# Attention in written order: ScalarE evicts every transposed pair, one reciprocal and product per batch, bias tables on VectorE, more warming

## The chip, the cores and the metric

One core of one Trainium2 chip runs the whole program. The metric is the device time of one execution in microseconds (us); lower is better. Engines: PE is TensorE, PEld its weight loads, DVE VectorE, ACT ScalarE, POOL GpSimd, SP SyncE, which here only issues DMAs.

## The reference

Attention over q, k, v of shape (2, 8, 768, 64), then a soft mixture of experts on the 1536 x 512 tokens, then a top-2 mixture of 8 experts. The change touches attention alone:

```
scores = scale * q @ k^T - slope_h * dist
keep   = (key < 8) | (0 <= row - key < 96)
a      = exp(scores - max) where keep, else 0
a      = a / (sum(a) + 1e-9)
out    = a @ v
```

A query sees the 8 global keys and the 96 keys up to itself, so a tile of 128 queries needs its own 128 keys and the 95 before them.

## The kernel before

Work is cut into 12 tiles of 128 queries, T = 0 to 11 (six for each batch element; m = T % 6 counts within it). A tile has 4 pairs of heads, n = 4 T + p. A pair is worked in two halves t of 64 queries: 128 rows (two heads by 64 queries) by 167 keys (95 before, 8 global, 64 own). Two pairs are a batch i = 0 to 23; two batches are a tile. All in float32.

For a pair, `scores` (L194) multiplies on TensorE into a buffer of PSUM (two of them), and VectorE adds the bias table, scales and takes each row's minimum in one instruction per half (L205, the reduction). `exps` (L209): ScalarE's exponential with the row's sum, one per half. `norm` (L216): GpSimd adds 1e-9 to the sums of the pair (L219), VectorE takes the reciprocal (L220), GpSimd multiplies the 2 x 167 columns by it into the padded tile Pb (L223), and where m > 0 the 8 global columns once more (L225). `turn` (L227): TensorE transposes Pb in blocks of 128 x 128 into PSUM tile pt. `turned` (L236) evicts pt to PT: the first pair of a batch on ScalarE (L241), the second on VectorE (L243). `values` (L248): PT times v into px. `valued` (L262): ScalarE evicts px to xT (L266); GpSimd keeps the first 8 rows of v. `stX` (L272): TensorE transposes xT back (L276), VectorE evicts to xs (L282). Where m = 0 there is no earlier tile, and half the transposes and values fall away.

After tiles 3, 7, 10 and 11 a segment (`logits` L289, `seg` L297) adds the tiles to the first mixture's running sums: logits on TensorE (L293), their maximum on VectorE, Et = exp on ScalarE, transposes of Et and of the logits (L325, L326), and U's product (L349) and update (L353). `seg` is a generator: each `next` issues one more step.

Inside attention the order on TensorE, VectorE, ScalarE and GpSimd is written out by hand in `attention_near` (L384), and every engine follows its queue in order. Pass i of the loop (L394) issues in this order: loads; the VectorE eviction for batch i-2; scores and exponentials of batch i; stX of the tile before on even i; values of batch i-2; valued on odd i; logits; norm of batch i; transposes of batch i-1 and the ScalarE eviction. Steps of a running segment (s1, s2) stand between them.

SP issues the loads in the written order too: v for tile T+1, q for T+2, k for T+3 at each even pass, then pieces of the first mixture's weights (512 KB each, 32 in all) as `PACE` allows (L24: pieces issued by pass i). A load waits until the buffer that it fills is free: 3 for q, 4 for v. The next expert weights (L618) use the memory that attention gives back. The bias tables (slope times distance, for m = 0 and m > 0) are built before the loop: four pieces on ScalarE (L389), four on GpSimd (L391). `NWARM` matmuls on zeros run at the start (L132).

Of the kernel before, what the change touches and what calls it, by code (L numbers as in the profile page):

```python
# [57 lines left out]
def emit(tc, d, near=True, stop=None):  # L58
    nc = tc.nc
    es = ExitStack()  # L60
    with es:
# [52 lines left out]
        ps_l = pool("ps_l", 1, s_ps, space=PSUM)  # L114
        ps_o = pool("ps_o", 1, s_ps, space=PSUM)

        NQ, NP = 3 if near else 2, 4
        qd = [ac.tile([128, 4, 2, 128], F32, name=f"qd{i}") for i in range(NQ)]
        if near:
            kx = ac.tile([128, 4, KP + 6 * KS], F32, name="kx")  # L120
            bias = ac.tile([128, 2, 4, 2, 167], F32, name="bias")
            Pb = [ac.tile([128, 2, 264], F32, name=f"Pb{i}") for i in range(NP)]
            gvt = lo.tile([8, 512], F32, name="gv")
        phis = lo.tile([128, 4, 32], F32, name="phis")
        if near:
            for nm, shape in (("Tt", [128, 2, 167]), ("vt", [128, 512])):
                wk.tile(shape, F32, name=nm, bufs=4)
# [41 lines left out]
        if near:  # L169
            s_hand = ExitStack()  # L170
            s_hand.enter_context(tc.manual_schedule(engines=hands))
            zero32 = wz.bitcast(F32)

            def clear(i, eng):
                for h in range(2):
                    eng(qd[i][64 * h:64 * h + 64, :, 1 - h, :], zero32[64 * h:64 * h + 64, 0:128].unsqueeze(1).to_broadcast([64, 4, 128]))

            by_act = lambda o, z: nc.scalar.activation(o, z, AF.Copy)
# [12 lines left out]

        S = {}

        def scores(n, st, nm):  # L194
            T, p = divmod(n, 4)
            m = T % 6
            s = ps_s.tile([128, 2, 167], F32, name="s")
            qv = qd[T % NQ].rearrange("p a h (c t) -> p a t (h c)", t=2)
            for t in range(2):
                a = KS * m + 64 * t  # L200
                nc.tensor.matmul(s[:, t, :], qv[:, p, t, :], kx[:, p, a:a + 167], start=True, stop=True)  # L201
            Tt = wk.tile([128, 2, 167], F32, name="Tt", bufs=4)
            for t in range(2):
                k = 2 * (p % 2) + t
                nc.vector.tensor_tensor_reduce(Tt[:, t], s[:, t], bias[:, int(m == 0), p, t], -0.125, 1e30, ALU.add, ALU.min,  # L205
                                               nm[:, k:k + 1])
            S[n] = Tt

        def exps(n, st, nm):  # L209
            Tt = S[n]  # L210
            for t in range(2):
                k = 2 * (n % 2) + t
                nc.scalar.activation(Tt[:, t], Tt[:, t], AF.Exp, bias=nm[:, k:k + 1], scale=-1.0,  # L213
                                     accum_out=st[:, k:k + 1])

        def norm(n, st):  # L216
            Pu, k = S[n], 2 * (n % 2)
            r = sm.tile([128, 2], F32, name="r")
            nc.gpsimd.tensor_scalar(r, st[:, k:k + 2], 1e-9, None, ALU.add)  # L219
            nc.vector.reciprocal(r, r)  # L220
            Pn = Pb[n % NP]
            wide = lambda t, c, step, w: bass.AP(t[:, 0, c:c + 1].tensor, t[:, 0, c:c + 1].offset, [t.ap[0], [step, 2], [1, w]])
            nc.gpsimd.tensor_tensor(wide(Pn, 33, 264 + 64, 167), Pu, r.unsqueeze(2).to_broadcast([128, 2, 167]), ALU.mult)  # L223
            if n // 4 % 6:
                nc.gpsimd.tensor_tensor(Pn[:, :, 0:8], wide(Pu, 95, 167 - 64, 8), r.unsqueeze(2).to_broadcast([128, 2, 8]), ALU.mult)  # L225

        def turn(n):  # L227
            c0 = 0 if n // 4 % 6 else 1
            Pn = Pb[n % NP]
            pt = ps_t.tile([128, 2, 2, 128], F32, name="pt")  # L230
            for ch in range(c0, 2):
                for t in range(2):
                    nc.tensor.transpose(pt[:, ch, t], Pn[:, t, 136 * ch:136 * ch + 128], ident)  # L233
            S[n] = pt

        def turned(n, act):  # L236
            c0 = 0 if n // 4 % 6 else 1
            pt = S[n]
            PT = lo.tile([128, 2, 2, 128], F32, name="PT", bufs=2)
            if act:  # L240
                nc.scalar.activation(PT[:, c0:], pt[:, c0:], AF.Copy)  # L241
            else:
                nc.vector.tensor_copy(PT[:, c0:], pt[:, c0:])  # L243
            S[n] = PT

        X = {}

        def values(n):  # L248
            T, p = divmod(n, 4)
            m = T % 6  # L250
            PT = S.pop(n)
# [132 lines left out]
        def attention_near():  # L384

            NB = 24
            all_units()
            for p in range(4):
                nc.scalar.activation(bias[:, 1, p], dist[1], AF.Copy, scale=negs[:, p:p + 1])  # L389
            for p in range(4):  # L390
                nc.gpsimd.tensor_scalar(bias[:, 0, p], dist[0], negs[:, p:p + 1], None, ALU.mult)  # L391
            part = {}
            segs = {}
            for i in range(NB + 3):  # L394
                T, u = divmod(i, 2)
                old = segs.get(T - 3) if u else segs.get(T - 4 + 1)
                new = i < NB
                if new and u == 0 and T >= 2:
                    if T + 1 < NT:
# [15 lines left out]
                a, b = divmod(i - 5, 2)  # L415
                s1 = segs.get(a) if b == 0 else None
                a, b = divmod(i - 6, 2)
                s2 = segs.get(a) if b == 0 else None
                if s2:
                    list(s2)  # L420
                if s1:
                    next(s1)
                if new:
                    st, nm = [sm.tile([128, 4], F32, name=k, bufs=3) for k in ("st", "nm")]
                    for n in (2 * i, 2 * i + 1):
                        scores(n, st, nm)
                    exps(2 * i, st, nm)
                if s1:
                    next(s1)
                if new:  # L430
                    exps(2 * i + 1, st, nm)
# [9 lines left out]
                if s1:  # L441
                    next(s1)
                if new:
                    norm(2 * i, st)
                    norm(2 * i + 1, st)
                if 0 <= i - 1 < NB:
                    for n in (2 * (i - 1), 2 * (i - 1) + 1):
                        turn(n)
                    turned(2 * (i - 1), True)
# [4 lines left out]
                if s1:  # L454
                    next(s1)
                    next(s1)
            more_w(2 * (NWA + NW))
            psl = logits(*SEGS[NT - 1])
            stX(NT - 1)
# [1149 lines left out]
```

## Time and profile before

| what | value |
|---|---|
| median of 3 runs | 394.22 us (392.58 to 397.57) |
| profiled execution | 394.14 us, of which span 391.9 us |
| busy in the span | PE 325.3, DVE 207.5, ACT 203.5, POOL 154.1 us |
| mean granted clock of TensorE | 0.941 of full |

The span runs from the first to the last instruction; the execution's own time has 2.24 us around it. In an order of time, a row gives start, duration, engine, line, operation, what it writes and reads, a count where several rows were merged, and in brackets how long the engine stood idle before and who ended that. Durations of pipelined matmuls overlap, so the distance between two starts tells more than a duration. A row of windows gives each engine's busy time in the stretch and its instructions, the mean granted clock (1.00 is full speed), the busy share of the DMA engines and GB/s. A row of groups gives busy time, mean ns of one instruction, and idle time before them.

### The profile page before, as it was taken

The page shows a single profiled execution, that of the slowest core. Times are in us where ns is not written, and L with a number is a line of the kernel's source. Part 1 is how long each engine was busy: PE and PEld are TensorE (multiplying, and loading weights), DVE is VectorE, ACT ScalarE, POOL GpSimd, SP SyncE. Part 2 cuts the span into 40 slices and gives each one's busy share as a digit, 9 for nine tenths or more (in the row PEclk, how much of TensorE's full clock was granted, in tenths as well). Part 3 has the DMA queues.
Part 4 walks back from the last instruction along what each step waited for, and adds up shares of the span by engine and source line. Part 5 has one row for each costly group of instructions (what it writes and reads, how often), then busy time and mean ns, then how long its engine had stood idle before and what let it go on. Part 6 is the DMA issues. An engine that isn't in the chain of part 4 may idle for free.

```text
span 391.9 us, 7690 instructions
## 1 busy us (share of the span) xinstructions
PE 325.3 (83%) x2680; PEld 190.8 (49%) x2680; DVE 207.5 (53%) x770; ACT 203.5 (52%) x476; POOL 154.1 (39%) x254
## 2 busy tenths in 40 slices
PE   5598989897978999969779798999993499999920
PEld 3486767675854433436344344454541255544410
DVE  2355556655445200378959474947580475995100
ACT  4375665654642210456747757768462665775200
POOL 4866664563630000203821533543615332341231
PEclk8699999998999999989999899999998599999985
DMA  7999997998299999990767899889686983233442
GB/s 185 266 316 324 290 300 237 281 330 281 73 323 359 375 397 388 393 387 22 243 137 238 246 267 343 261 203 315 156 256 140 261 248 42 32 34 49 55 52 33
DMA packets 49515, 89.52 MB, mean 228 GB/s; under 512 B 3408, under 2 KB 18384, under 8 KB 49472
## 3 DMA queue, kind: packets, MB, share of 16 engines
q1 hardware_dynamic: 44992, 81.40, 62.9%
q0 software_dynamic: 4480, 7.57, 13.4%
q8 instruction: 23, 0.38, 0.4%
q14 instruction: 20, 0.16, 0.1%
HBM read 78.35 MB, written 10.62 MB: 227 GB/s over the span
## 4 chain that ended last, share of the span: by engine, by line
PE 47%; DVE 18%; DMA 12%; POOL 8%; issue 7%; ACT 5%; SPq 1%; POOLq 0%; DVEq 0%; ACTq 0%
PE y L1152 20%; PE y L699 4%; POOL Pb L223 3%; DMA out_y<-ys,sidx 3%; PE pg L653 3%; PE h L653 3%; DMA out_y<-w,sidx 2%; PE s L201 2%; DVE Tt L205 2%; PE h L1074 2%; DMA cT<-ctab,gidx 2%; PE px L259 2%; DVE hh L1083 2%; PE y L723 2%; ACT Tt L213 2%
## 5 line engine op out<-in xcount | busy, mean ns | idle before, releaser
L1152 PE MATMUL y<-w2hl,hh 128*128 128x512 f16 x552 | 128.4, 386 | 1.9 <-ACT hh L1075 1.9
L1152 PEld LDWEIGHTS <-hh 128*128 128x128 f16 x552 | 53.3, 99 | 65.2 <-issue 6.7
L213 ACT ACTIVATE Tt<-Tt,nm 128x167 f32<-128x167 f32 x96 | 40.5, 423 | 41.1 <-DVE nm L205 32.3
L1161 POOL DMA_INDIRECT out_y<-ys,sidx x16 | 27.2, 1698 | 64.0 <-ACT ys L1158 24.6
L1083 DVE SCALAR_TENSOR_TENSOR hh<-h,hh 128x512 f16<-128x512 f32 x46 | 29.6, 685 | 41.6 <-ACT hh L1075 41.6
L223 POOL TENSOR_TENSOR Pb<-Tt,r 128x334 f32<-128x334 f32 x48 | 35.7, 744 | 16.0 <-DVE r L220 15.0
L201 PE MATMUL s<-kx,qd 128*128 128x167 f32 x192 | 35.1, 331 | 2.9 <-DMA qd<-in_qt 2.9
L201 PEld LDWEIGHTS s<-kx,qd 128*128 128x128 f32 x192 | 31.3, 214 | 6.4 <-issue 6.2
L259 PE MATMUL px<-PT,vt 128*64 128x128 f32 x352 | 28.2, 287 | 5.2 <-DVE PT L243 4.1
L1161 POOL DMA_INDIRECT out_y<-c,sidx x8 | 15.7, 1960 | 42.9 <-ACT hh L1075 20.0
L220 DVE RECIPROCAL r<-r 128x2 f32<-128x2 f32 x48 | 7.9, 165 | 44.7 <-POOL r L219 44.6
L1075 ACT ACTIVATE hh<-h 128x512 f16<-128x512 f32 x46 | 24.9, 591 | 10.7 <-PE h L1074 10.7
L1171 POOL DMA_INDIRECT cT<-ctab,gidx x23 | 25.6, 1112 | 11.9 <-issue 5.5
L205 DVE CUSTOM_DVE_ANT_0 Tt<-s,bias 128x167 f32<-128x167 f32 x96 | 26.3, 327 | 7.2 <-ACT bias L389 5.9
L233 PE MATMUL pt<-c,Pb 128*128 128x128 f32 x176 | 25.4, 286 | 4.5 <-POOL Pb L223 4.5
L766 ACT ACTIVATE w2hl<-w 128x1024 f16<-128x1024 f32 x20 | 20.9, 1049 | 12.3 <-DMA w<-in_w2b 12.3
L259 PEld LDWEIGHTS px<-PT,vt 128*64 128x64 f32 x352 | 18.7, 138 | 13.2 <-DVE PT L243 8.2
L233 PEld LDWEIGHTS pt<-c,Pb 128*128 128x128 f32 x176 | 19.3, 144 | 8.9 <-POOL Pb L223 5.1
L780 ACT ACTIVATE w2hl<-w,pmw 128x1024 f16<-128x1024 f32 x19 | 20.9, 1142 | 3.2 <-DVE pmw L754 2.5
L786 DVE SCALAR_TENSOR_TENSOR w2hl<-w,pmw,w2hl 128x1024 f16<-128x1024 f32 x18 | 22.5, 1279 | 0.1
L219 POOL TENSOR_SCALAR r<-st 128x2 f32<-128x2 f32 x48 | 10.4, 218 | 20.0 <-ACT Tt L213 17.3
L1158 ACT ACTIVATE ys<-y,gsc 128x512 f32<-128x512 f32 x16 | 10.9, 683 | 14.0 <-PE y L1152 14.0
(280 smaller groups left out, 519.6 us busy)
## 6 DMA issues: line engine op xcount, KB each, us to landing
w<-in_w2b SPq DMA_DIRECT2D x10, 1024.0 KB, 6.3
w<-in_w1a SPq DMA_DIRECT2D x16, 512.0 KB, 7.3
w<-in_w2a SPq DMA_DIRECT2D x16, 512.0 KB, 6.6
w<-in_w1a SPq DMA_DIRECT2D x8, 1024.0 KB, 9.8
w<-in_w2a SPq DMA_DIRECT2D x8, 1024.0 KB, 13.1
w<-in_w1b SPq DMA_DIRECT2D x8, 1024.0 KB, 6.5
w2hl<-in_w1b SPq DMA_DIRECT2D x8, 1024.0 KB, 10.2
w2hl<-in_w2b SPq DMA_DIRECT2D x6, 1024.0 KB, 7.5
```

What stands on the lines that cost most here:

```text
L201: nc.tensor.matmul(s[:, t, :], qv[:, p, t, :], kx[:, p, a:a + 167], start=True, stop=True)
L205: nc.vector.tensor_tensor_reduce(Tt[:, t], s[:, t], bias[:, int(m == 0), p, t], -0.125, 1e30, ALU.add, ALU.min, nm[:, k:k + 1])
L213: nc.scalar.activation(Tt[:, t], Tt[:, t], AF.Exp, bias=nm[:, k:k + 1], scale=-1.0, accum_out=st[:, k:k + 1])
L223: nc.gpsimd.tensor_tensor(wide(Pn, 33, 264 + 64, 167), Pu, r.unsqueeze(2).to_broadcast([128, 2, 167]), ALU.mult)
L233: nc.tensor.transpose(pt[:, ch, t], Pn[:, t, 136 * ch:136 * ch + 128], ident)
L259: nc.tensor.matmul(px[64 * h:64 * h + 64, p, :], vv[:, c:c + 64], PT[:, ch, :, 64 * h:64 * h + 64], start=(ch == 0 or m == 0), stop=(ch == 1))
L653: nc.tensor.matmul(psum[32 * g:32 * g + 32, 0:n], lhs(k), rhs_of(k, g), start=(k == 0), stop=(k == nk - 1), tile_position=(0, 32 * g))
L1075: nc.scalar.activation(hh[:, 0, 4 * q:4 * q + 4], ph, AF.Relu)
L1083: nc.vector.scalar_tensor_tensor(hh[:, 1, 4 * q:4 * q + 4], phs[q], 0.0, hh[:, 0, 4 * q:4 * q + 4], ALU.max, ALU.subtract)
L1152: nc.tensor.matmul(py, hh[:, hx, f], w2hl[:, e, wx, f], start=(n == 0), stop=(n == 23))
L1161: nc.gpsimd.indirect_dma_start(out=out, out_offset=bass.IndirectOffsetOnAxis(ap=sidx[:, j:j + 1], axis=0), in_=ys, in_offset=None, compute ...
L1171: nc.gpsimd.indirect_dma_start(out=cg[n], out_offset=None, in_=ctab, in_offset=bass.IndirectOffsetOnAxis(ap=gidx[:, n:n + 1], axis=0))
```

## The change

All transposed pairs are evicted by ScalarE, right after their transposes in `turn`; xT is evicted by VectorE instead of ScalarE. A batch has one tile Tt of 4 x 167 columns (two buffers), one sum + 1e-9, one reciprocal of four columns and one product of 4 x 167 columns into one of two batch-wide Pb tiles. In a pass, the scores of both pairs come first, then four exponentials; the norm of batch i comes after the transposes of batch i-1. The steps of a segment are issued in the pass of its logits and the next one. The bias tables are built by VectorE, all but one piece, most of them after the first scores. 16 warming matmuls stand in place of 7, and 12 and 3 more in passes 1 and 2. An exponential on zeros is issued at the start. `PACE` gives 4 pieces in 3 passes in place of 3 in 2.

```
-NWARM = 7
+NWARM = 16
-PACE = lambda i: 1 + 3 * i // 2
+PACE = lambda i: 1 + 4 * i // 3
+FILL = {1: 12, 2: 3}
...
-        NQ, NP = 3 if near else 2, 4
+        NQ, NP = 3 if near else 2, 2
...
-            Pb = [ac.tile([128, 2, 264], F32, name=f"Pb{i}") for i in range(NP)]
+            Pb = [ac.tile([128, 4, 264], F32, name=f"Pb{i}") for i in range(NP)]
...
             nc.vector.memset(kx[:, :, 0:KP], 0.0)
+            nc.scalar.activation(sm.tile([128, 4], F32, name="st", bufs=3), zero32[:, 0:4], AF.Exp)
             clear(1, by_dve)
...
+        def scores(i, nm):
+            Tt = wk.tile([128, 4, 167], F32, name="Tt", bufs=2)
+            for n in (2 * i, 2 * i + 1):
...
+        def exps(i, st, nm):
+            Tt = S[i]
+            for k in range(4):
+                nc.scalar.activation(Tt[:, k], Tt[:, k], AF.Exp, bias=nm[:, k:k + 1], scale=-1.0,
                                      accum_out=st[:, k:k + 1])
...
+        def norm(i, st):
+            Pu = S[i]
+            r = sm.tile([128, 4], F32, name="r", bufs=3)
+            nc.gpsimd.tensor_scalar(r, st, 1e-9, None, ALU.add)
             nc.vector.reciprocal(r, r)
+            Pn = Pb[i % NP]
...
+            nc.gpsimd.tensor_tensor(wide(Pn, 33, 264 + 64, 528, 167), Pu.rearrange("p (a t) c -> p a t c", t=2), rb(167), ALU.mult)
+            if i // 2 % 6:
+                nc.gpsimd.tensor_tensor(Pn[:, :, 0:8].rearrange("p (a t) c -> p a t c", t=2), wide(Pu, 95, 167 - 64, 334, 8), rb(8), ALU.mult)
...
-        def turned(n, act):
...
+            PT = lo.tile([128, 2, 2, 128], F32, name="PT", bufs=2)
+            nc.scalar.activation(PT[:, c0:], pt[:, c0:], AF.Copy)
+            X["PT", n] = PT
...
-            nc.scalar.activation(X["xT", T], X["px"], AF.Copy)
+            nc.vector.tensor_copy(X["xT", T], X["px"])
...
-            for p in range(4):
-                nc.scalar.activation(bias[:, 1, p], dist[1], AF.Copy, scale=negs[:, p:p + 1])
-            for p in range(4):
-                nc.gpsimd.tensor_scalar(bias[:, 0, p], dist[0], negs[:, p:p + 1], None, ALU.mult)
+            def tables(m, a, b):
+                nc.vector.tensor_tensor(bias[:, m, a:b].rearrange("p a t c -> p a (t c)"),
+                                        dist[m].rearrange("p t c -> p (t c)").unsqueeze(1).to_broadcast([128, b - a, 334]),
+                                        negs[:, a:b].unsqueeze(2).to_broadcast([128, b - a, 334]), ALU.mult)
+            def fill(k):
+                for _ in range(k):
+                    nc.tensor.matmul(pw, wz[:, 0:128], wz, start=True, stop=True)
+            nc.scalar.activation(bias[:, 1, 0], dist[1], AF.Copy, scale=negs[:, 0:1])
+            tables(1, 1, 2)
...
-                if 0 <= i - 2 < NB:
-                    turned(2 * (i - 2) + 1, False)
...
+                s1 = segs.get(T - 2) if u else None
+                if new:
+                    st, nm = [sm.tile([128, 4], F32, name=k, bufs=3) for k in ("st", "nm")]
+                    scores(i, nm)
+                    exps(i, st, nm)
+                if i == 0:
+                    tables(1, 2, 4)
+                if i == 1:
+                    tables(0, 0, 2)
+                if i == 2:
+                    tables(0, 2, 4)
+                fill(FILL.get(i, 0))
                 if s1:
                     next(s1)
+                    next(s1)
                 if u == 0 and 0 <= T - 2 < NT - 1:
                     stX(T - 2)
                 if 0 <= i - 2 < NB:
...
                     if u:
                         valued(T - 1)
+                if s1:
+                    list(s1)
                 if u == 0 and T - 2 in SEGS and T - 2 < NT - 1:
                     segs[T - 2] = seg(*SEGS[T - 2], logits(*SEGS[T - 2]))
...
                 if 0 <= i - 1 < NB:
                     for n in (2 * (i - 1), 2 * (i - 1) + 1):
                         turn(n)
+                if new:
+                    norm(i, st)
+                if u == 0 and T - 2 in segs:
+                    next(segs[T - 2])
+                    next(segs[T - 2])
```

## Rows read from the trace of the kernel before

**Rows 1.** Windows: from the scores of batch 4 to those of batch 23.

```profile
24.19:106.29 82.10, 73.33 (x710) 59.59 (x709) 46.22 (x233) 49.13 (x189) 47.97 (x122) 0.98 0.88 271
```

**Rows 2.** TensorE in order of time: passes 21 and 22, and the tail.

```profile
99.11 1.31 PE L201 MATMUL s<-kx,qd 128*128 128x167 f32 x8
...
102.30 1.31 PE L201 MATMUL s<-kx,qd 128*128 128x167 f32 x8
103.44 0.60 PE L276 MATMUL o<-c,xT 128*128 128x128 f32 x4
...
106.29 1.31 PE L201 MATMUL s<-kx,qd 128*128 128x167 f32 x8
...
119.19 1.04 PE L293 MATMUL psl<-xT,phis 128*32 128x128 f32 x8
```

**Rows 3.** VectorE in order of time: one steady pass.

```profile
79.60 0.17 DVE L220 RECIPROCAL r<-r 128x2 f32<-128x2 f32 x1 [1.40 <-POOL r L219]
79.69 0.69 DVE L243 COPY PT<-pt 128x512 f32<-128x512 f32 x1
80.29 0.32 DVE L205 CUSTOM_DVE_ANT_0 Tt<-s,bias 128x167 f32<-128x167 f32 x1
...
83.66 0.17 DVE L220 RECIPROCAL r<-r 128x2 f32<-128x2 f32 x1 [1.34 <-POOL r L219]
```

**Rows 4.** ScalarE, then GpSimd, in order of time: the same pass.

```profile
80.71 0.43 ACT L213 ACTIVATE Tt<-Tt,nm 128x167 f32<-128x167 f32 x1 [1.70 <-POOL Pb L223]
...
82.40 0.57 ACT L266 ACTIVATE xT<-px 128x512 f32<-128x512 f32 x1
...
81.91 0.22 POOL L219 TENSOR_SCALAR r<-st 128x2 f32<-128x2 f32 x1
82.41 0.74 POOL L223 TENSOR_TENSOR Pb<-Tt,r 128x334 f32<-128x334 f32 x1 [0.28 <-DVE r L220]
```

**Rows 5.** TensorE in order of time: the first segment.

```profile
51.53 1.08 PE L293 MATMUL psl<-xT,phis 128*32 128x128 f32 x32
...
57.40 0.30 PE L325 MATMUL psl<-c,Et 128*128 128x128 f32 x1 [1.60 <-DVE r L220]
...
59.21 1.06 PE L349 MATMUL o<-xs,Ek 128*32 128x512 f32 x8 [0.52 <-DVE Ek L330]
```

**Rows 6.** Groups by line and shape, first 130 us.

```profile
L223 POOL TENSOR_TENSOR Pb<-Tt,r 128x334 f32<-128x334 f32 x48 | 35.7, 744 | 16.0 <-DVE r L220 15.0 <-PE s L201 0.7 <-PE pt L233 0.3
L241 ACT ACTIVATE PT<-pt 128x512 f32<-128x512 f32 x20 | 11.7, 584 | 5.0 <-PE pt L233 5.0
L225 POOL TENSOR_TENSOR Pb<-Tt,r 128x16 f32<-128x16 f32 x40 | 8.7, 218 | 0.0
L629 DVE TENSOR_TENSOR cx<-Ltok,cm 128x384 f32<-128x384 f32 x1 | 0.6, 558 | 0.0
```

**Rows 7.** GpSimd, then TensorE, in order of time: the start.

```profile
9.40 4.47 POOL L391 TENSOR_SCALAR bias<-xs,negs 128x334 f32<-128x334 f32 x4 [4.53 <-DMA qd<-in_qt]
...
1.20 3.11 PE L132 MATMUL o<-xT 128*128 128x512 f16 x7 [1.20 <-DVE xT L129]
7.22 4.22 PE L201 MATMUL s<-kx,qd 128*128 128x167 f32 x16 [2.92 <-DMA qd<-in_qt]
...
17.08 2.43 PE L201 MATMUL s<-kx,qd 128*128 128x167 f32 x8
...
24.19 1.31 PE L201 MATMUL s<-kx,qd 128*128 128x167 f32 x8
```

**Rows 8.** Windows: during the scores of batch 2.

```profile
17.20:18.20 1.00, 1.00 (x6) 1.00 (x6) 0.17 (x1) 0.89 (x5) 0.72 (x2) 0.50 1.07 324
```

**Rows 9.** Windows: transfers in attention, at its end, and behind it.

```profile
20.00:65.00 45.00, 40.67 (x392) 33.20 (x388) 25.32 (x128) 27.45 (x106) 27.89 (x72) 0.99 1.00 309
100.00:107.60 7.60, 7.45 (x73) 6.35 (x74) 3.97 (x22) 5.00 (x19) 4.74 (x12) 1.00 0.07 23
110.00:175.00 65.00, 56.61 (x627) 27.70 (x626) 22.89 (x118) 18.88 (x49) 7.75 (x22) 0.97 1.02 386
```

More of the change, by code (lines that the diff above doesn't have):

```diff
@@ L125, in emit @@
         if near:
-            for nm, shape in (("Tt", [128, 2, 167]), ("vt", [128, 512])):
-                wk.tile(shape, F32, name=nm, bufs=4)
+            wk.tile([128, 4, 167], F32, name="Tt", bufs=2)
+            wk.tile([128, 512], F32, name="vt", bufs=4)
         wz = wk.tile([128, 512], F32, name="xT", bufs=NX).bitcast(F16)[:, 0:512]
@@ L192, in emit @@
         S = {}
[L194 to L213, printed above, removed]
+        X = {}
+        def scores(i, nm):
+            Tt = wk.tile([128, 4, 167], F32, name="Tt", bufs=2)
+            for n in (2 * i, 2 * i + 1):
+                T, p = divmod(n, 4)
+                m = T % 6
+                s = ps_s.tile([128, 2, 167], F32, name="s")
+                qv = qd[T % NQ].rearrange("p a h (c t) -> p a t (h c)", t=2)
+                for t in range(2):
+                    a = KS * m + 64 * t
+                    nc.tensor.matmul(s[:, t, :], qv[:, p, t, :], kx[:, p, a:a + 167], start=True, stop=True)
+                for t in range(2):
+                    k = 2 * (p % 2) + t
+                    nc.vector.tensor_tensor_reduce(Tt[:, k], s[:, t], bias[:, int(m == 0), p, t], -0.125, 1e30, ALU.add, ALU.min,
+                                                   nm[:, k:k + 1])
+            S[i] = Tt
@@ L214, in exps @@
+        def exps(i, st, nm):
+            Tt = S[i]
+            for k in range(4):
+                nc.scalar.activation(Tt[:, k], Tt[:, k], AF.Exp, bias=nm[:, k:k + 1], scale=-1.0,
                                      accum_out=st[:, k:k + 1])
[L216 to L219, printed above, removed]
+        def norm(i, st):
+            Pu = S[i]
+            r = sm.tile([128, 4], F32, name="r", bufs=3)
+            nc.gpsimd.tensor_scalar(r, st, 1e-9, None, ALU.add)
@@ L220, in norm @@
             nc.vector.reciprocal(r, r)
[L221 to L225, printed above, removed]
+            Pn = Pb[i % NP]
@@ new lines, in wide @@
+            def wide(t, c, step, pair, w):
+                a = t[:, 0, c:c + 1]
+                return bass.AP(a.tensor, a.offset, [t.ap[0], [pair, 2], [step, 2], [1, w]])
+            rb = lambda w: r.rearrange("p (a t) -> p a t", t=2).unsqueeze(3).to_broadcast([128, 2, 2, w])
+            nc.gpsimd.tensor_tensor(wide(Pn, 33, 264 + 64, 528, 167), Pu.rearrange("p (a t) c -> p a t c", t=2), rb(167), ALU.mult)
+            if i // 2 % 6:
+                nc.gpsimd.tensor_tensor(Pn[:, :, 0:8].rearrange("p (a t) c -> p a t c", t=2), wide(Pu, 95, 167 - 64, 334, 8), rb(8), ALU.mult)
@@ L227, in turn @@
         def turn(n):
             c0 = 0 if n // 4 % 6 else 1
-            Pn = Pb[n % NP]
+            Pn = Pb[n // 2 % NP]
             pt = ps_t.tile([128, 2, 2, 128], F32, name="pt")
@@ L232, in turn @@
                 for t in range(2):
[L233 to L246 removed]
+                    nc.tensor.transpose(pt[:, ch, t], Pn[:, 2 * (n % 2) + t, 136 * ch:136 * ch + 128], ident)
+            PT = lo.tile([128, 2, 2, 128], F32, name="PT", bufs=2)
+            nc.scalar.activation(PT[:, c0:], pt[:, c0:], AF.Copy)
+            X["PT", n] = PT
         def values(n):
@@ L250, in values @@
             m = T % 6
-            PT = S.pop(n)
+            PT = X.pop(("PT", n))
             if p == 0:
@@ L387, in attention_near @@
             all_units()
-            for p in range(4):
-                nc.scalar.activation(bias[:, 1, p], dist[1], AF.Copy, scale=negs[:, p:p + 1])
-            for p in range(4):
-                nc.gpsimd.tensor_scalar(bias[:, 0, p], dist[0], negs[:, p:p + 1], None, ALU.mult)
-            part = {}
+            def tables(m, a, b):
[7 more added lines that the diff above has]
+            tables(1, 1, 2)
             segs = {}
@@ L395, in attention_near @@
                 T, u = divmod(i, 2)
-                old = segs.get(T - 3) if u else segs.get(T - 4 + 1)
                 new = i < NB
@@ L412, in attention_near @@
                     more_w(PACE(i))
-                if 0 <= i - 2 < NB:
-                    turned(2 * (i - 2) + 1, False)
[L415 to L420, printed above, removed]
+                s1 = segs.get(T - 2) if u else None
[10 more added lines that the diff above has]
+                fill(FILL.get(i, 0))
                 if s1:
                     next(s1)
[L423 to L428, printed above, removed]
                     next(s1)
-                if new:
-                    exps(2 * i + 1, st, nm)
                 if u == 0 and 0 <= T - 2 < NT - 1:
@@ L438, in attention_near @@
                         valued(T - 1)
+                if s1:
+                    list(s1)
                 if u == 0 and T - 2 in SEGS and T - 2 < NT - 1:
                     segs[T - 2] = seg(*SEGS[T - 2], logits(*SEGS[T - 2]))
[L441 to L445, printed above, removed]
                 if 0 <= i - 1 < NB:
@@ L453, in attention_near @@
                     nc.gpsimd.memset(U, 0.0)
-                if s1:
-                    next(s1)
-                    next(s1)
             more_w(2 * (NWA + NW))
```

2 lines of the change are left out of this document (removed).

## The prediction

> **What bounds the kernel now.** I read the stages first, then each engine's order of time in one steady stretch, then the two ends of attention. The change touches only attention, which fills the first 119 us of a span of 391.9. Between the scores of batch 4 at 24.19 us and those of batch 23 at 106.29 lie 19 passes of the loop in 82.1 us, 4.3 us each. TensorE shows 73.3 us busy there, ScalarE 49.1, GpSimd 48.0 and VectorE 46.2, at a mean granted clock of 0.98 [rows 1]. But busy TensorE hides waiting. Where it runs without a gap, a pass on an odd batch takes 3.19 us (scores 99.11 to scores 102.30) and an even one has 0.60 more for the transposes of the finished tile (L276): two passes, one tile, 6.98 us [rows 2].
>
> What holds the steady pass at four is a ring through VectorE [rows 3, 4]. The second reciprocal of a batch starts at 79.60; behind it in VectorE's queue stands the eviction of the second transposed pair (79.69), and only behind that the reductions of the next scores (80.29). Then ScalarE's exponentials (80.71), GpSimd's sum + 1e-9 (81.91), a reciprocal, the product (82.41), and all this once more for the second pair, whose reciprocal starts at 83.66. The ring is 4.06 us; TensorE, at 3.19 to 3.79, waits inside it. Twice a slot segment adds a stall: TensorE idles 1.60 us before the transposes of Et, and 0.52 before U's product [rows 5].
>
> **The change part by part.** Names: p is the time at which TensorE starts the scores of a batch.
>
> *The ring.* The eviction leaves VectorE, and one reciprocal serves four rows of statistics. New ring: reductions to first exponential 0.42 (80.29 to 80.71); four exponentials at 0.42 and the last sum, to 82.40, 1.69 [rows 4]; the sum + 1e-9 and the reciprocal, at most 0.50 together (81.91 to the product at 82.41): about 2.6 us. It no longer decides; TensorE's 3.19 is late next.
>
> *The product.* GpSimd took 744 ns for 334 columns and 218 ns for 16 [rows 6]: 1.65 ns a column and 0.19 fixed. One product of 668 columns is then 1.30 us, at most 2 x 0.744 = 1.49, and the 32-column one 0.25. From p: scores of the first pair and semaphore 0.7, first exponential 1.12, last sum 2.9 (it waits for the second pair's reductions), reciprocal 3.2, product 3.5 to 4.8, small product 5.05. TensorE comes to these transposes one pass later, after that pass's scores (1.14), L276 (0.60, in one of the two passes) and values (half of the 2.05 left of 3.19): 3.19 + 0.60 + 1.14 + 1.0 = 5.9 after p. 0.8 us of slack.
>
> *The two evictions on ScalarE.* One is 584 ns [rows 6], some 0.5 behind another. ScalarE's pass is 1.69 + 1.1 = 2.8 us. In order, the evictions stand behind the exponentials of the batch, wait for the transposes that end TensorE's pass, and the next exponentials stand behind them: first eviction about when the first transposes end, second done 0.8 us into the next pass, next exponentials wanted at 1.12. It fits with 0.3 us. What waits behind a late one is everything: exponentials, product, transposes. Closed over two passes: exponentials to product end 4.0, transposes and evictions 1.6, so 5.6 us for two; TensorE has 6.98.
>
> *xT to VectorE.* 0.69 us by the 128x512 copy at 79.69 [rows 3], every second pass, from about p+2.4, before the reciprocal at p+3.2: covered.
>
> *Segments.* Logits, transposes and U keep their TensorE time, 1.08 + 0.30 + 1.06 [rows 5] = 2.4 us for each of the two in this stretch; the steps are spread over two passes. I count 0.6 us each for a reciprocal that now stands behind U's update.
>
> So the 19 passes: 10 even x 3.79 + 9 odd x 3.19 = 66.6; the two batches of the tile that starts the second sequence have half the transposes and values: -2 x 1.0 = -2.0; segments 2 x 3.0 = +6.0; hand-offs +0.4 (an estimate, 0.02 each). **71.0 us for 82.1: -11.1.** Bounds: TensorE alone 69.4; the ring kept, 82.
>
> *The start.* GpSimd built four bias tables from 9.40 for 4.47 us, in its queue ahead of the first sum + 1e-9 [rows 7]. They move to VectorE as products of two SBUF tensors, not seen in this form; nearest, 384 columns in 558 ns [rows 6]: 334 take 0.5 and 668 about 1.0, between 0.7 (no fixed part) and 1.9 (GpSimd's price doubled). I take 1.0. First scores still wait for their queries at 7.22. Then, by the offsets from p above: reductions 8.0 to 9.1; tables 9.1 to 10.1; statistics of batch 0 ready 10.3, product 10.9 to 12.2; batch 1's exponentials 11.1 to 12.8; 12 filling matmuls to about 12.3; transposes; batch 2's scores 13.2; its tables 15 to 16; batch 3's scores 16.0, after batch 1's transposes; batch 2's product ends at 18.3 and its transposes at 19.4, and batch 4's scores follow them. Against 24.19: **-4.8**. The table load moves ahead of the data; scores not starting before 7.22, I give it nothing.
>
> This rests on the clock. The seven warming matmuls took 3.11 us, 0.43 us apart, and at 17.2 to 18.2 the granted clock was 0.50, the lower level, 1.2 GHz [rows 7, 8]; batch 2's scores lasted 2.43 us there, against 1.14 later. Nine more matmuls and 15 fillers keep TensorE active from 1.2 to past 12 with a gap under 1 us; at 0.43 us apart the 16 end at 8.1. If the clock stays low until about 13, the fillers cost 12 x 0.21 = 2.6 more and the scores of batch 1 some 0.7: start -1.5, not -4.8.
>
> Against the move of the tables stands a rule of the Trainium skill, "SBUF — State Buffer", the section on SBUF's two sides: a VectorE instruction with two SBUF inputs and a GpSimd one that reads SBUF exclude each other for the whole instruction. No row of before has such a pair in attention. By the rule two tables would meet the product of batches 0 and 1, and the later of them would wait out the other: the total would be about 1 us later, 379.
>
> *The tail.* From batch 23's scores at 106.29 to the last logits at 119.19 are 12.9 us [rows 2]. In their place: this pass 3.2; L276, values, logits and transposes 3.6; evictions, then Et and the segment's transposes 1.7; values, xT and U 2.3: 10.8, **-2.1**.
>
> *Transfers.* SP's order is kept; 4 pieces of weights in 3 passes replace 3 in 2. Before, 271 GB/s x 82.1 us = 22.2 MB passed in the stretch; at the 309 GB/s that the busy queues gave from 20 to 65 us, that is 72 us, against my 71: just enough, since the last weights aren't needed there (the queues stood near idle, 23 GB/s, from 100 to 107.6). Bounds: 271 would hold the old time, 386 (the later rate) would need 58 [rows 9]. Behind attention, expert weights stream at 386 GB/s without a break to 175. This stream starts when attention's buffers come free, at batch 23, and so moves by 15.9 us while the products move by 18: I charge **+1.5**.
>
> Sum against the profiled execution (394.14 us: its span and 2.24 around it): 394.14 - 4.8 - 11.1 - 2.1 + 1.5 = 377.6, call it **378.0 us**. The median of the runs shown, 394.22, is the same within 0.1.
>
> **The rivals.**
> 1. *Transfers become attention's pace.* For it: the share of the queues is 1.00 at 309 GB/s already. Against: weights can be late. At 290 GB/s the 22.2 MB take 76.6 us, 5.6 more: 383.5.
> 2. *The ring comes back through ScalarE.* Its evictions wait at TensorE's last step, with 0.3 us to spare; if each batch's hand-offs cost 0.6 us more than I count, a pass stays at four. Start and tail alone: 394.1 - 6.9 + 1.5 = 389. Against: the hand-off from the reciprocal to the product is 0.28 [rows 4], and 0.6 would have to be added to a pass with slack at every step.
> 3. *The warming doesn't lift the clock in time:* 394.1 - 1.5 - 11.1 - 2.1 + 1.5 = 381. For it: it didn't before. Against: at 24.19 batch 4's scores took 1.31 us, so it came before that, under less activity [rows 7].
> 4. *GpSimd becomes the bound, and the kernel slower.* Its pass is the product + 0.8 us (0.50 to the product, 0.25 for the small one). At a product of 3.25 us it equals the old pass of 4.06, and from 3.55 on it eats the 7 us won at the ends; the price at three times my value, 3.9 us: 24 x 0.65 = 15.6 us more, less 7: 403. For it: no row has this pattern of four dimensions. Against: two rows of 8 columns cost no more than 218 ns, so a row of the pattern costs little by itself.
>
> **How the numbers follow.** Forecast 0.60; transfers 0.13; ScalarE's ring 0.12; low clock 0.09; GpSimd 0.06. A measurement of this kernel tells about 2%, 7.9 us: under 386.3 is faster. Forecast, transfers and clock lie below it (0.82, less 0.03 for several of them together), a fifth of the ring's cases too: 0.81. Between: 0.13. Slower: 0.06. The low end is TensorE alone (69.4, 1.6 less), no charge behind (1.5 less) and 2 us more at each end of attention: 371. The high end takes in rivals 1 and 3 and most of 2: 389.
>
> **What would show it.** Right: no VectorE PT copy; reciprocals of four columns, 24 of them; passes of 3.2 and 3.8 us with TensorE's idle before L259 gone; batch 4's scores near 19.4, batch 23's near 90.4; GpSimd's big product near 1.3 us; last logits near 101. Wrong: TensorE waiting for Pb or PT every pass, scores waiting for kx or qd, a granted clock of 0.50 after 13 us, or MoE products that wait for weights by more than 2 us.

## The result, and the profile after

**376.88 us** median (375.67 to 379.35, four runs), beside 395.60 (392.58 to 397.57) for the kernel before on the same chip: a ratio of 0.954 [0.946, 0.963], faster. In a later session with five rounds it was 375.24 against 392.75, 0.952 [0.947, 0.957]. The forecast was 378.0. The profiled execution of after took 379.35 us (span 377.4). Medians here and below are of all executions, while ratios leave out those over 1.5% slower than the fastest of their kernel, so a ratio isn't always that of the two medians.

| stage, us | before | forecast | after |
|---|---|---|---|
| scores of batch 4 start | 24.19 | 19.4 | 19.62 |
| 19 passes, to the scores of batch 23 | 82.10 | 71.0 | 69.77 |
| tail, to the last logits | 12.90 | 10.8 | 11.68 |
| last logits start | 119.19 | about 101 | 101.07 |
| first product h behind attention | 125.39 | | 108.08 |
| end of the span | 391.9 | | 377.4 |

Windows of after: the 19 passes (compare [rows 1]), the end of attention and the stretch behind it (compare [rows 9]), and 5 us about the last logits. Columns: stretch, length, busy time and instructions of PE, PEld, DVE, ACT and POOL, granted clock, share of the DMA engines, GB/s.

```profile
19.62:89.39 69.77, 68.26 (x710) 59.07 (x709) 40.51 (x205) 53.97 (x197) 37.67 (x67) 1.00 1.07 302
92.00:157.00 65.00, 56.79 (x623) 27.65 (x622) 21.36 (x109) 18.43 (x47) 7.52 (x19) 0.95 1.04 400
100.00:105.00 5.00, 4.54 (x23) 2.50 (x18) 2.50 (x12) 1.30 (x5) 0.81 (x3) 0.73 1.02 398
```

In the passes TensorE is busy 68.26 of 69.77 us: the stage now runs at TensorE's own pace. What is left of its waiting there, by the view of waits (who waited for whom: sum, times, longest):

```profile
PE psl L322 <- DVE Lsb L319: 0.8, 2, 0.4
PE pt L240 <- POOL Pb L232: 0.6, 1, 0.6
```

TensorE of after in order of time, to compare with [rows 2, 5, 7]: the start, two steady passes, the first segment, the tail, and one product behind attention.

```profile
1.19 6.55 PE L133 MATMUL o<-xT 128*128 128x512 f16 x16 [1.19 <-DVE xT L130]
7.58 1.30 PE L205 MATMUL s<-kx,qd 128*128 128x167 f32 x8
...
10.36 2.75 PE L393 MATMUL o<-xT 128*128 128x512 f16 x12
...
26.45 1.31 PE L205 MATMUL s<-kx,qd 128*128 128x167 f32 x8
27.60 0.60 PE L273 MATMUL o<-c,xT 128*128 128x128 f32 x4
28.13 1.09 PE L256 MATMUL px<-PT,vt 128*64 128x128 f32 x16
29.16 1.09 PE L240 MATMUL pt<-c,Pb 128*128 128x128 f32 x8
30.09 1.31 PE L205 MATMUL s<-kx,qd 128*128 128x167 f32 x8
...
33.28 1.31 PE L205 MATMUL s<-kx,qd 128*128 128x167 f32 x8
...
46.46 0.30 PE L322 MATMUL psl<-c,Et 128*128 128x128 f32 x1 [0.42 <-DVE Lsb L319]
...
98.05 0.27 PE L322 MATMUL psl<-c,Et 96*128 96x96 f32 x1 [1.78 <-DVE rs L325]
...
99.36 1.93 PE L346 MATMUL o<-xs,Ek 128*32 128x512 f32 x6
101.07 1.85 PE L290 MATMUL psl<-xT,phis 128*32 128x128 f32 x8
...
135.03 1.07 PE L650 MATMUL h<-w,siT 128*32 128x256 f32 x16 [0.60 <-DMA w<-in_w1a]
```

A pass on an even batch takes 3.64 us (26.45 to 30.09), an odd one 3.19 (to 33.28), each without a gap. The three engines around it in the same passes, first VectorE, then ScalarE, then GpSimd (compare [rows 3, 4]):

```profile
26.70 0.18 DVE L222 RECIPROCAL r<-r 128x4 f32<-128x4 f32 x1 [0.37 <-POOL r L221]
...
27.34 0.33 DVE L208 CUSTOM_DVE_ANT_0 Tt<-s,bias 128x167 f32<-128x167 f32 x1 [0.46 <-PE s L205]
...
29.89 0.18 DVE L222 RECIPROCAL r<-r 128x4 f32<-128x4 f32 x1 [0.86 <-POOL r L221]
```

```profile
27.77 0.43 ACT L215 ACTIVATE Tt<-Tt,nm 128x167 f32<-128x167 f32 x1 [0.41 <-DVE nm L208]
...
29.91 1.09 ACT L242 ACTIVATE PT<-pt 128x512 f32<-128x512 f32 x2 [0.36 <-PE pt L240]
```

```profile
26.96 1.30 POOL L230 TENSOR_TENSOR Pb<-Tt,r 128x668 f32<-128x668 f32 x1 [0.29 <-DVE r L222]
28.22 0.24 POOL L232 TENSOR_TENSOR Pb<-Tt,r 128x32 f32<-128x32 f32 x1
...
29.64 0.22 POOL L221 TENSOR_SCALAR r<-st 128x4 f32<-128x4 f32 x1 [1.18 <-ACT Tt L215]
```

The reader is to see two things. Nothing stands between a reciprocal and the next reductions in VectorE's queue, where [rows 3] had a PT copy. And each of the three waits in nearly every pass for the engine ahead of it (DVE for s or r, ACT for nm, POOL for Tt or r): all have some slack, ScalarE the 0.41 us ahead of its first exponential. The groups of attention by line and shape give the sizes of the new instructions:

```profile
L230 POOL TENSOR_TENSOR Pb<-Tt,r 128x668 f32<-128x668 f32 x24 | 31.2, 1299 | 9.4 <-DVE r L222 9.1 <-PE s L205 0.4
L242 ACT ACTIVATE PT<-pt 128x512 f32<-128x512 f32 x40 | 21.8, 595 | 10.4 <-PE pt L240 10.1
L232 POOL TENSOR_TENSOR Pb<-Tt,r 128x32 f32<-128x32 f32 x20 | 4.8, 240 | 0.0
```

### The profile page after: what moved, and what is told of

It is laid out like the page before. It is cut to its first block, busy times and chain, and to the rows that moved or that the text cites. A ratio compares the mean times of both kernels' runs of the same rounds, so it can differ in the third digit from the quotient of the medians.

```text
span 377.4 us, 7576 instructions
## 1 busy us (share of the span) xinstructions
PE 325.8 (86%) x2704; PEld 191.5 (51%) x2704; DVE 203.8 (54%) x738; ACT 208.2 (55%) x486; POOL 135.1 (36%) x180
## 3 DMA queue, kind: packets, MB, share of 16 engines
HBM read 78.35 MB, written 10.62 MB: 236 GB/s over the span
## 4 chain that ended last, share of the span: by engine, by line
PE 58%; DMA 16%; DVE 13%; ACT 4%; issue 4%; POOL 1%; SPq 0%; DVEq 0%; POOLq 0%; ACTq 0%
PE y L1149 19%; PE s L205 6%; PE px L256 6%; PE pt L240 6%; DMA w<-in_w1a 4%; DMA w<-in_w2b 3%; PE pg L650 3%; DMA out_y<-w,sidx 2%; PE y L696 2%; DVE hh L1080 2%; DMA w<-in_w1b 2%; DVE w2hl L783 2%; PE h L1071 2%; DMA cT<-ctab,gidx 2%; PE o L133 2%
## 5 line engine op out<-in xcount | busy, mean ns | idle before, releaser
L1158 POOL DMA_INDIRECT out_y<-ys,sidx x16 | 26.3, 1642 | 65.4 <-ACT ys L1155 19.7
L230 POOL TENSOR_TENSOR Pb<-Tt,r 128x668 f32<-128x668 f32 x24 | 31.2, 1299 | 9.4 <-DVE r L222 9.1
L205 PE MATMUL s<-kx,qd 128*128 128x167 f32 x192 | 31.5, 306 | 0.2 <-DVE nm L208 0.2
L242 ACT ACTIVATE PT<-pt 128x512 f32<-128x512 f32 (+1 forms) x48 | 24.4, 558 | 10.4 <-PE pt L240 10.1
L205 PEld LDWEIGHTS s<-kx,qd 128*128 128x128 f32 x192 | 28.0, 196 | 0.6 <-DVE nm L208 0.5
L240 PE MATMUL pt<-c,Pb 128*128 128x128 f32 x176 | 24.4, 280 | 1.1 <-POOL Pb L232 1.0
L256 PE MATMUL px<-PT,vt 128*64 128x128 f32 x352 | 24.5, 279 | 0.0
L1155 ACT ACTIVATE ys<-y,gsc 128x512 f32<-128x512 f32 x16 | 10.9, 682 | 14.0 <-PE y L1149 14.0
L215 ACT ACTIVATION_READ_ACCUMULATOR Tt<-Tt,nm 128x1 f32 x96 | 17.9, 187 | 0.0
```

The source lines that it names most:

```text
L215: nc.scalar.activation(Tt[:, k], Tt[:, k], AF.Exp, bias=nm[:, k:k + 1], scale=-1.0, accum_out=st[:, k:k + 1])
L230: nc.gpsimd.tensor_tensor(wide(Pn, 33, 264 + 64, 528, 167), Pu.rearrange("p (a t) c -> p a t c", t=2), rb(167), ALU.mult)
L240: nc.tensor.transpose(pt[:, ch, t], Pn[:, 2 * (n % 2) + t, 136 * ch:136 * ch + 128], ident)
L1158: nc.gpsimd.indirect_dma_start(out=out, out_offset=bass.IndirectOffsetOnAxis(ap=sidx[:, j:j + 1], axis=0), in_=ys, in_offset=None, compute ...
```

## The experiments

The theory: the 11 us of the passes come from breaking the ring, and the PT eviction and the two reciprocals a batch each belong to it. Rivals: it is the new written order as a whole; it is the start alone, or the warming. Then the places where the forecast was thin: GpSimd's slack, the clock, the tables, the tail, the weights. Three sessions, each with its own runs of before. Ratios are against those. The stages come from one profiled execution of each kernel; they are steadier than the totals, since the part behind attention, which no kernel here changes, took between 267.1 and 276.3 us from the last logits to the end of the span, with before at 272.7.

**1 and 2. The start alone, and the loop alone.** The first is the kernel before with the new start; the second is after with the old start.

```diff
# start_only: before, and
-NWARM = 7
+NWARM = 16
+FILL = {1: 12, 2: 3}
+            nc.scalar.activation(sm.tile([128, 4], F32, name="st", bufs=3), zero32[:, 0:4], AF.Exp)
-            for p in range(4):
-                nc.scalar.activation(bias[:, 1, p], dist[1], AF.Copy, scale=negs[:, p:p + 1])
-            for p in range(4):
-                nc.gpsimd.tensor_scalar(bias[:, 0, p], dist[0], negs[:, p:p + 1], None, ALU.mult)
+            nc.scalar.activation(bias[:, 1, 0], dist[1], AF.Copy, scale=negs[:, 0:1])
+            tables(1, 1, 2)
...
+                if i == 0:
+                    tables(1, 2, 4)
...
+                fill(FILL.get(i, 0))
# loop_only: after with all of this turned back
```

> The kernel before with the new start alone (16 warming matmuls, 12 and 3 fillers, bias tables on VectorE, the early exponential). My theory, that the start is a term of its own: batch 4's scores near 20 us in place of 24.19, the 19 passes behind it 82 us as before, total about 390. Rival, that the start only pays together with the new loop: batch 4's scores after 23, total 393 to 394.

> The changed kernel with the old start (7 warming matmuls, no fillers, tables on ScalarE and GpSimd). My theory: batch 4's scores near 24, the 19 passes still 69.8 us, total about 381. Rival, that the steady passes need the warmer start: passes of more than 71 us, total above 383.

Measured: start_only 386.23 us, 0.985 [0.979, 0.991]; batch 4 at 20.35, passes 79.96. loop_only 373.85 us, 0.962 [0.954, 0.970]; batch 4 at 23.43, passes 69.76, tail 10.90. Start and loop are separate: the start brings 3.8 us ahead of the passes, and the loop brings its 12.3 in them with the old start too. The passes of start_only are 2.1 us shorter than before's with the same loop. Most of this isn't the start. In before's profile the granted clock fell behind the second segment's wait, in start_only's it didn't: U's product there, first in before, with the clock of the stretch, then in start_only.

```profile
92.74 1.88 PE L349 MATMUL o<-xs,Ek 128*32 128x512 f32 x8 [0.52 <-DVE Ek L330]
...
90.00:100.00 10.00, 8.54 (x61) 6.34 (x62) 4.75 (x20) 4.86 (x20) 3.84 (x12) 0.83 0.93 279
```

```profile
88.40 1.06 PE L351 MATMUL o<-xs,Ek 128*32 128x512 f32 x8 [0.52 <-DVE Ek L332]
```

From this product to the scores of batch 21 are 6.37 us in before (92.74 to 99.11) and 4.73 in start_only (88.40 to 93.13). So about 1.6 of the 12.3 us are a fall of the clock that this one profile of before had, and not work of the new loop.

**3, 4 and 5. The ring, one edge at a time, then both.** One kernel gives the odd pair's eviction back to VectorE, ahead of the next reductions as before; one gives each pair its own sum + 1e-9, reciprocal and products; the third does both.

```diff
# evict_dve: odd pairs, issued before scores(i) of the next pass
-            nc.scalar.activation(PT[:, c0:], pt[:, c0:], AF.Copy)
+                nc.vector.tensor_copy(PT[:, c0:], pt[:, c0:])
# pair_norm: in norm(), for each pair a
-            r = sm.tile([128, 4], F32, name="r", bufs=3)
+            for a in range(2):
+                r = sm.tile([128, 2], F32, name="r")
...
# both_undone: both
```

> The changed kernel with the second pair of each batch evicted by VectorE ahead of the next reductions, as before; one reciprocal and product per batch stay. My theory, that the old ring needs both the eviction and the second reciprocal in it: the ring stays under TensorE's pass, the 19 passes take 70 to 72 us, total within 2 us of the changed kernel. Rival, that the eviction on VectorE alone was the bound: 76 to 82 us, total 384 to 390.

> The changed kernel with a sum, a reciprocal and a product for each pair, as before; evictions stay on ScalarE. My theory: the second pair's product ends about when the batch's did (the first pair's starts 0.9 us earlier), the 19 passes take 70 to 72 us, total within 2 us of the changed kernel. Rival, that the batch-wide reciprocal is what pays: 76 us or more, total 383 or more.

> The changed kernel with both undone: the second pair evicted by VectorE ahead of the next reductions, and a reciprocal and product for each pair. My theory, the ring: reciprocal, eviction, reductions, exponentials, product, second reciprocal close again at about four us, the 19 passes take 79 to 82 us, total about 388, though each of the two alone costs little. Rival, that the written order of the passes brought the gain: 70 to 73 us, total under 380.

Measured: evict_dve 372.93 us, 0.958 [0.952, 0.965], passes 70.41 (0.6 more than after), tail 10.21. pair_norm 378.07, 0.971 [0.964, 0.978], passes 72.27 (2.5 more, a little over the 70 to 72 expected), tail 13.06. both_undone 385.10, 0.987 [0.978, 0.997], passes **80.65** (10.9 more). The two edges cost 3.1 us one at a time and 10.9 together. TensorE of both_undone at both ends of the passes, then VectorE in order of time, with the ring of [rows 3] back:

```profile
20.07 1.31 PE L205 MATMUL s<-kx,qd 128*128 128x167 f32 x8
...
100.72 1.31 PE L205 MATMUL s<-kx,qd 128*128 128x167 f32 x8
```

```profile
33.88 0.17 DVE L225 RECIPROCAL r<-r 128x2 f32<-128x2 f32 x1 [1.40 <-POOL r L224]
33.96 0.69 DVE L248 COPY PT<-pt 128x512 f32<-128x512 f32 x1
34.56 0.32 DVE L208 CUSTOM_DVE_ANT_0 Tt<-s,bias 128x167 f32<-128x167 f32 x1
...
37.87 0.17 DVE L225 RECIPROCAL r<-r 128x2 f32<-128x2 f32 x1 [1.33 <-POOL r L224]
```

From reciprocal to reciprocal are 3.99 us (4.06 before), in the new written order and with the new start. TensorE's largest waits in its passes:

```profile
PE px L262 <- DVE PT L248: 5.7, 12, 0.9
PE psl L328 <- DVE Lsb L325: 1.7, 2, 0.9
...
```

So the rival "the order as a whole" falls: with the order kept and the ring closed again, 1.4 of the 12.3 us remain, no more than the clock in before's profile accounts for, and start_only, with the old loop and the new start, has 79.96. In pair_norm the ring lacks the copy, but ScalarE still waits behind the second reciprocal (0.66 us for nm at 33.77). Its long tail holds a fall of the clock as well (U's product takes 1.93 us in it), so the tail doesn't tell what the edge costs there. In evict_dve the tail is shorter than where ScalarE evicts (10.85 with the clock kept), which pays back the 0.6 us of the passes: once a batch has one reciprocal, no difference clear of the intervals remains between the two engines for the eviction.

**6 and 7. GpSimd's slack.** The small product done three times (0.48 us more in each batch that has one), and the big one twice.

```diff
# small_thrice
+                for _ in range(3):
                     nc.gpsimd.tensor_tensor(Pn[:, :, 0:8].rearrange("p (a t) c -> p a t c", t=2), wide(Pu, 95, 167 - 64, 334, 8), rb(8), ALU.mult)
# product_twice
+            for _ in range(2):
                 nc.gpsimd.tensor_tensor(wide(Pn, 33, 264 + 64, 528, 167), Pu.rearrange("p (a t) c -> p a t c", t=2), rb(167), ALU.mult)
```

> The changed kernel with GpSimd's small product (32 columns) issued three times, 0.48 us more per batch. My theory, that the product has 0.6 us of slack before TensorE's transposes: no change, the 19 passes 69.8 to 70.5 us. Rival, that GpSimd is on the path: 8 us more.

> The changed kernel with GpSimd's product of 668 columns issued twice, 1.26 us more per batch. My theory: 0.6 us of it is covered, each tile of two passes grows from 6.83 to about 7.5 us, the 19 passes by 6 to 7, total 383 to 385. Rival, GpSimd on the path with all of it: 24 us more, total 401. Rival, much more slack: no change.

Measured: small_thrice 376.56 us, 0.962 [0.953, 0.971]; passes 70.69, 0.9 more for 17 times 0.48 (batches 12 and 13 have no small product). product_twice 386.05, 0.986 [0.976, 0.997]; passes 76.87, 7.1 more, a little over the 6 to 7 expected. TensorE's waits for Pb in the passes of product_twice:

```profile
PE pt L241 <- POOL Pb L233: 5.5, 13, 1.2
PE pt L241 <- POOL Pb L231: 1.3, 1, 1.3
```

The first 0.48 us cost about a tenth of themselves, and the 1.3 us of a second product cost TensorE a wait in most passes (13 of 19). In after itself a small product ends at 28.46 (28.22 + 0.24) and the transposes that read it start at 29.16: the slack is 0.7 us, a little under the 0.8 of the prediction. Even a product of twice the size leaves the kernel no slower than before.

**8 and 9. The warming.** After with 7 warming matmuls and no fillers, and with 1 and no fillers.

```diff
# cold_start
-NWARM = 16
+NWARM = 7
-FILL = {1: 12, 2: 3}
+FILL = {}
# no_warm: NWARM = 1, FILL = {}
```

> The changed kernel with 7 warming matmuls and no fillers; tables stay on VectorE. My theory, that the warming holds the clock up: granted clock 0.50 in the scores of batches 0 to 2, batch 4's scores 1.5 to 3.3 us later than 19.62. Rival, that the tables alone brought the start's gain and the fillers only fill idle time: batch 4's scores within 0.5 us of 19.62.

> The changed kernel with one warming matmul in place of 16 and no fillers. My theory after the cold start's run, that the tables on VectorE bring the start's gain and a low clock hides behind the product of batch 0: batch 4's scores within 1 us of 19.6 and the total within 2 us of the changed kernel. Rival, that the clock stays low until batch 4 without warming: 2 to 4 us later.

Measured: cold_start 374.84 us, 0.961 [0.952, 0.971], batch 4 at 19.58. no_warm 373.88, 0.947 [0.941, 0.954], batch 4 at 19.05. TensorE of no_warm in order of time:

```profile
6.34 4.85 PE L205 MATMUL s<-kx,qd 128*128 128x167 f32 x16 [4.54 <-DMA qd<-in_qt]
12.33 0.66 PE L240 MATMUL pt<-c,Pb 128*128 128x128 f32 x4 [1.14 <-POOL Pb L230]
...
98.77 1.06 PE L346 MATMUL o<-xs,Ek 128*32 128x512 f32 x6
```

The 16 scores run at half pace (0.30 us apart, 0.16 later), and it costs nothing: TensorE then waits 1.14 us for GpSimd's first product anyway. Warming and fillers are worth nothing here that can be measured. cold_start against loop_only differs only in the tables and the early exponential: 19.58 against 23.43, so these two together carry the start, 3.85 us. Which of the two it is, the traces tell (see the start, below).

**10 to 12. The tail and the weights.** The change once more, beside a kernel with the old `PACE` and ten matmuls that fill TensorE's wait in the tail, and that kernel with evict_dve.

```diff
# pace_tail
-PACE = lambda i: 1 + 4 * i // 3
+PACE = lambda i: 1 + 3 * i // 2
+                if i == NB + 1:
+                    for _ in range(10):
+                        nc.tensor.matmul(ph, hot[:, 0:128], hot[:, 0:334], start=True, stop=True)
# after_again: the change as it is; evict_pace_tail: pace_tail and evict_dve
```

> The changed kernel once more, beside the next three on one chip: ratio near 0.954, batch 4's scores near 19.6 us, the 19 passes 69.8, expert products (first to last of the first mixture) 34 us with a wait of 0.6 to 1.2 for weights.

> The changed kernel with the old pace of the weights (3 pieces in 2 passes) and ten matmuls of 334 columns where TensorE idles 1.8 us before the last full segment's transposes. My theory, that the leftover pieces delay the stream of expert weights: the first mixture's products take 33.4 us in place of 34.2 and attention's passes stay at 69.8 to 70.3; the fill keeps the clock at 1.00 from 95 to 105 us; 1 to 2 us less in all. Rival, that attention needs the slower pace: scores wait for q or k, passes of 72 us or more. Rival, that the stream is bound by its bytes: products 34 us as before.

> The pace and the fill of the kernel before last, and the second pair's eviction on VectorE. Meant as the best version: passes 70.4, tail 10.2 to 10.8, products 33.4: ratio 0.945 to 0.953. If the eviction on VectorE costs more than it gives back at the tail, no better than the kernel with pace and fill alone.

Measured: after_again 375.24 us, 0.952 [0.947, 0.957]. pace_tail 374.60, 0.952 [0.947, 0.957], tail 10.85. evict_pace_tail 376.97, 0.958 [0.954, 0.963], outside the 0.945 to 0.953 expected; tail 10.37. TensorE of pace_tail: the filler, U's product, and the product that waits for weights.

```profile
95.25 1.58 PE L432 MATMUL s<-c 128*128 128x334 f16 x10
...
98.50 1.06 PE L346 MATMUL o<-xs,Ek 128*32 128x512 f32 x6
...
133.17 1.07 PE L655 MATMUL h<-w,siT 128*32 128x256 f32 x16 [1.23 <-DMA w<-in_w1a]
```

The filler keeps U's product at 1.06 us (1.93 in after and in after_again), and the tail is 0.8 shorter; but in no_warm and cold_start it was 1.06 without any filler, so this is a matter of the run as well. The older pace doesn't change the passes either (69.74). Whether it changes the wait for weights can't be told: the wait is 1.23 us here and 0.60 in after, but none in after_again, which is the same program as after, and 2.5 in all in small_thrice. No version beats the change by more than the intervals allow; no_warm is the simplest that equals it.

## Why the prediction was right

**The ring (right, and shown).** It predicted that the VectorE copy and the second reciprocal of a batch close a ring of 4.06 us, and that TensorE's 3.19 is late next. both_undone brings it back at 3.99 us, and the 19 passes at 80.65 us; without it TensorE has 3.19 and 3.64. The new chain was put at 2.6 us and took 2.8: 2.55 from the reductions at 27.34 to the reciprocal at 29.89, and 0.26 from a reciprocal to its product (26.70 to 26.96). It stays under 3.19.

**The passes (69.77 for 71.0).** Five terms were off, by both signs, and they sum to the 1.2 us. An even pass has 0.45 us more than an odd one, not 0.60: the duration of four grouped matmuls (0.60) is longer than the step to the next instruction, and the prediction took the duration, 10 x 0.15 = 1.5 too much. The hand-offs of 0.4 aren't there. The two segments take 2.8 us each, not 3.0: the two passes of the first are 4.64 and 5.01 us (40.10 to 44.74 to 49.75) where 3.64 and 3.19 are steady. Their stall is another than the one named: 0.42 us ahead of the transposes of Et, not a reciprocal behind U, which starts at 49.62 and holds nothing. Against these stand two terms: the passes with half the transposes and values save 1.5 us, not 2.0, and TensorE waits once for Pb, 0.56 us at 61.53, where the second sequence starts and a pass is shorter; the slack of 0.8 was worked out for a full one.

**The product and the evictions (right).** 1299 ns for 1.30 us, 240 for 0.25, 595 for 0.58. ScalarE's evictions behind an even batch's exponentials wait 0.36 us for the transposes, and the next exponentials wait 0.41 for nm, so rival 2 had no ground. For rival 4, product_twice has a product of 2.6 us and the passes still 5 us under the old ones.

**The start (-4.57 for -4.8: right for part of the reason).** The move of the tables out of GpSimd's queue brings it, as the sum had it. The early exponential isn't it: in loop_only, without it, batch 0's exponentials end at 10.37 us, in after at 10.63, but the sum + 1e-9 that needs them starts at 13.82 in loop_only, behind GpSimd's tables (9.27 to 13.74), and at 10.80 in after. The clock was up in time in after (8 scores in 1.30 us at 7.58), but that doesn't matter to the start. Rival 3 charged 0.7 us for batch 1's scores at the lower level; cold_start and no_warm show that GpSimd's first product hides this. Its larger part, 2.6, was the price of the fillers themselves at the low clock; without fillers and warming there is none. That price, fillers at a low clock, no run here had.

**The tables against the product.** Four tables of 668 columns, from three runs, show what stands in their way. VectorE and GpSimd of after, and VectorE and GpSimd of product_twice and no_warm, in order of time:

```profile
9.48 0.85 DVE L387 TENSOR_TENSOR bias<-xs,negs 128x668 f32<-128x668 f32 x1
...
12.21 1.14 DVE L387 TENSOR_TENSOR bias<-xs,negs 128x668 f32<-128x668 f32 x1
...
11.35 1.29 POOL L230 TENSOR_TENSOR Pb<-Tt,r 128x668 f32<-128x668 f32 x1 [0.30 <-DVE r L222]
```

```profile
16.21 1.56 DVE L388 TENSOR_TENSOR bias<-xs,negs 128x668 f32<-128x668 f32 x1
...
10.62 3.16 POOL L231 TENSOR_TENSOR Pb<-Tt,r 128x668 f32<-128x668 f32 x2 [0.30 <-DVE r L222]
...
14.38 2.68 POOL L231 TENSOR_TENSOR Pb<-Tt,r 128x668 f32<-128x668 f32 x2 [0.30 <-DVE r L222]
```

```profile
14.70 0.89 DVE L387 TENSOR_TENSOR bias<-xs,negs 128x668 f32<-128x668 f32 x1
...
13.59 1.30 POOL L230 TENSOR_TENSOR Pb<-Tt,r 128x668 f32<-128x668 f32 x1 [0.30 <-DVE r L222]
```

Alone a table takes 0.85 us (forecast 1.0). Where it starts during a product, it ends 0.70 to 0.71 us after that product's end, however long the overlap was: 12.64 to 13.35 (overlap 0.43), 17.06 to 17.77 (0.85), 14.89 to 15.59 (0.19). So it makes next to no headway until the product is done. In product_twice it also goes the other way: the pair at 10.62 takes 0.48 us longer than the pair at 14.38, and a table lies across its middle (11.49 to 12.63). The rule of the Trainium skill, "SBUF — State Buffer", the section on SBUF's two sides, says just this (whichever of the two starts first has the port for its whole instruction), and this case's trace agrees. The prediction had the rule's total at 1 us more; what failed is not the rule but the price. Of the two meetings that it counted, one took place in after. That table met the product late, so it lost 0.29 us, and VectorE then idled 0.34 us for the next reciprocal anyway: nothing on the path.

**The tail (11.68 for 10.8).** The clock was not in the sum. TensorE waits 1.78 us before the segment's transposes (96.27 to 98.05), then the granted clock falls (0.73 from 100 to 105, at the lower level of 1.2 GHz for part of it), and U's product takes 1.93 us instead of 1.06. With the clock kept, pace_tail, no_warm and cold_start have 10.85 or 10.86, the forecast, but partly by luck. By no_warm the stretch of Et and its transposes takes 2.1 us (95.68 to 97.75), not 1.7, and values, xT and U take 1.9 (to 99.65), not 2.3: two errors that cancel.

**Transfers (rival 1 false; the charge of 1.5 not separable).** The queues moved 302 GB/s through the passes, less than the 309 that the sum took, and TensorE waited for no kx or qd there. So 21.1 MB passed in place of 22.2; that what passed later was weights is argued from SP's order, not measured. Behind attention the last logits came 18.1 us earlier and the first h 17.3, and at 135.03 one h waits 0.60 us for w1a. In the profile 14.5 us are left at the end of the span, by the medians of the last session 17.5. From the last logits to the end of the span after has 276.3 and 273.2 us in two profiles, before 272.7, and all kernels 267.1 to 276.3: a charge of 1.5 lies inside this scatter. So it is partly chance that the median met the forecast within 1.1 us: the passes were 1.2 better than forecast, start and tail 0.2 and 0.9 worse, and the part behind varies by more than all of these.

The queues are now busy without a break from 5 us to 157 us, where [rows 9] had 23 GB/s at attention's end. That shortening attention further would pay little behind it, until fewer bytes pass, is argued from this, not shown; the waits for w1a are no steady sign of it, since some runs with attention as short have none.

## What to carry to other kernels

A wait that ends on a busy engine may be a ring: follow the releasers until the same instruction comes round again, one pass later, and compare that time with the pass of the engine that you want to be the bound. A ring gives way when its edges are cut far enough under that pass, so one edge put back alone doesn't tell what it is worth: here two edges cost 0.6 and 2.5 us each by itself, and 10.9 together. Work put in to raise the clock is worth checking against what its stage waits for: here the first product of another engine hid the lower clock entirely.

## What the runs showed of the hardware that was not expected

The granted clock of the profile doesn't tell the level at the very start. No_warm's window over its first 16 scores reads 1.00, and so does after's during its warming matmuls:

```profile
6.40:11.20 4.80, 4.79 (x16) 4.25 (x16) 2.44 (x13) 1.89 (x8) 0.46 (x2) 1.00 1.02 269
```

```profile
6.00:7.00 1.00, 1.00 (x4) 0.32 (x3) 0.00 (x0) 0.00 (x0) 0.00 (x0) 1.00 0.94 274
```

Yet the scores are 0.30 us apart there and 0.16 later, and 512 columns take 0.41 us (16 in 6.55) where the fillers take 0.23 (12 in 2.75): the lower level in both, as in [rows 7, 8], where 8 scores took 2.43 us (0.30 apart) at a granted 0.50. At the start the level is to be read from the distance of the matmuls, not from the clock's column. In after_again the same 16 took 4.96 us and in pace_tail 5.41, so the rise comes at another time in each run.

The same wait of 1.78 us in the tail is followed by a fall of the clock in after, after_again and pair_norm (U's product 1.93 us), and by none in no_warm, cold_start, small_thrice and product_twice (1.06).
